# Batch 0's loads ahead of the weights in a one-core linear attention and gated FFN kernel on Trainium2

## The chip, the cores and the metric

The kernel runs on one core of a Trainium2 chip. The metric is the device time of one execution in microseconds (us). Lower is better. Engines: PE is the matmul engine (PEld its weight loads), DVE the vector engine, ACT the scalar engine, POOL GpSimd, SP SyncE. POOL and SP also issue the DMAs here, each through a queue of its own.

## What is computed

```python
def phi(x): return np.where(x > 0, x, np.exp(x) - 1.0) + 1.0
# q, k, v: 8 batches, 8 heads, 576 rows, 64 columns, f32
q_p, k_p = phi(q), phi(k)
kv  = einsum('bhsd,bhse->bhde', k_p, v);  z = sum(k_p, axis=2)
x   = einsum('bhsd,bhde->bhse', q_p, kv) / (einsum('bhsd,bhd->bhs', q_p, z) + 1e-6)
# x is rearranged to 4608 tokens x 512
out = ((x @ w1) * (x @ w2)) @ w3 @ w_out        # w1, w2: 512x1024, w3: 1024x1024, w_out: 1024x512
```

Since nothing nonlinear stands between w3 and w_out, the kernel multiplies them once (the "fold", wf = w3 @ w_out, 1024 x 512) and then computes out = ((x @ w1) * (x @ w2)) @ wf.

## The kernel before

Each of the 576 rows of a batch is either one of 512 "main" rows (four to a partition) or one of 64 remainder rows; the remainder rows of two batches share 128 partitions. There are eight chunks of 512 tokens, one per batch, and a ninth chunk that gathers all remainder rows.

The order of the work is written out by hand: the string ORDER (L451 to L521) lists steps, and a loop at the end of the kernel calls them one after the other. Every engine takes its own instructions in that order and waits only for data and for buffers. A second string, GATES (L523), adds a wait of a load for the landing of another. The steps, with their arguments in the order of the string:

- Loads: ld:n,b,h0,nh,queue loads nh heads of q, k or v of batch b (L117); lr loads the remainder rows of one batch, lp those of two (L124, L132); l3:i loads tile i of w3 (128 rows, L155), lo two of the eight row blocks of w_out (L148), lw:n,x,w a range of columns of w1 or w2 (L141). Weight loads are issued on POOL and turn f32 into bf16 on the way. q, k, v arrive in a pool of five 1 MB buffers, which the two halves of w3 use too. A POOL load waits for the landing of the one eight before it.
- phi: x is the exponential (ACT, L164), t is max(x, 0) + 1 (DVE, L170), m takes the minimum of both (DVE, L177). xr, tr, mr do the same for the remainder.
- Attention of a batch: v and vr copy v to bf16; kv multiplies k and v for a pair of heads (PE, L230); kc and kh copy the result out; qt transposes q on PE and qc copies it out (later batches: qd, a DMA transpose); na multiplies q with kv (PE, L288); nd divides (three DVE instructions, L304); xp and xc transpose the result for the gates (later batches: xd).
- Fold: w3t transposes a tile of w3 on PE (L351), w3c copies it out; wa:c0,n multiplies one block c of all of the first four tiles with w_out (L368), so that four results grow side by side in two attention buffers of PSUM (pool at_ps, two buffers); wf:i does a later tile at once in a buffer of mm_ps (four buffers, L377); wc copies the result to SBUF.
- Gates and output: f:c,f multiplies chunk c with 128 columns of w1 and of w2 (eight matmuls, L397); ac copies the first product out (L405), ab multiplies it with the second (L410); fk does a part of f for the first gate of chunk 0. o:c,m gives 128 rows of the output (eight matmuls, L415), oc copies them out (L422), st stores them (L434); ol is the last output tile, done in two halves (L439). For chunk 8 one st is two stores.
- warm:n runs n matmuls on zeros.

In before the loads of the start stand in this order on POOL: tiles 0 to 3 of w3, w_out, tiles 4 and 5 of w3, then k, q and v of batch 0, tiles 6 and 7 of w3, the first, second and remaining columns of w1 and w2, then batch 1. All of the fold but tiles 6 and 7 is done on PE ahead of batch 0's attention, those two in the middle of it, and the gates of chunk 0 follow.

Of the kernel before, what the change touches and what calls it, by code (L numbers as in the profile page):

```python
# [8 lines left out]
F32 = mybir.dt.float32  # L9
# [4 lines left out]
P = 128  # L14
# [4 lines left out]
def kernel(  # L19
# [11 lines left out]
    nc = tc.nc  # L31
# [4 lines left out]
    FC = DFF // P  # L36
# [10 lines left out]
    ld = ctx.enter_context(tc.tile_pool(name="ld", bufs=5))  # L47
# [327 lines left out]
                ps["wf", i] = o[:, i % 2, :]  # L375

    @step  # L377
    def wf(i):
        o = got(ps, ("wf", i), mm_ps, [P, DM], F32, "mm", "wf_ps")
        for c in range(FC):  # L380
            nc.tensor.matmul(o, sb["w3t", i][:, c, :], sb["wo"][:, c, :],  # L381
                             start=(c == 0), stop=(c == FC - 1))
# [66 lines left out]
                queue.dma_start(out=dst[:, cols], in_=d[r, cols])  # L449

    ORDER = """  # L451
    const:0 const:2 lr:k,0,s const:9 l3:0 lr:v,0,s const:11 l3:1 warm:26,0 const:3 l3:2 l3:3 lo:0,2
    xr:k,0,0 const:6 lo:2,2 const:8 const:7 lo:4,2 zr:0,1 tr:k,0,0 lo:6,2 mr:k,0,0 const:10 l3:4 const:4
    const:1 l3:5 zr:0,0 const:5 w3t:0 ld:k,0,0,4,g warm:8,1 w3c:0,a w3t:1 warm:8,2 w3c:1,v vr:0,a
    ld:k,0,4,4,g w3t:2 warm:8,3 w3c:2,a w3t:3 ld:q,0,0,4,g warm:8,4 w3c:3,a ld:q,0,4,4,g wa:0,1 wa:1,1
    ld:v,0,0,4,g wa:2,1 wa:3,1 ld:v,0,4,2,g wa:4,1 wa:5,1 ld:v,0,6,2,g wa:6,1 l3:6 w3t:5 w3t:4 w3c:5,a
    wa:7,1 l3:7 t:k,0,0,4 w3c:4,a wf:5 wc:2,v wc:3,a wc:1,v lw:0,0,256 wc:0,a t:k,0,4,4 x:k,0,0,4 wf:4
    lw:1,0,256 wc:5,a m:k,0,0,0 m:k,0,0,1 x:q,0,0,4 warm:10,10 t:q,0,0,4 wc:4,a warm:10,11 lw:0,1,256
    m:q,0,0,1 x:q,0,4,4 m:q,0,0,0 warm:10,12 warm:10,13 x:k,0,4,4 lw:1,1,256 v:0,0,4,v qt:0,0,2
    m:k,0,4,3 lw:0,1,512 kv:0,1 qc:0,0,2,a m:k,0,4,2 kv:0,0 v:0,4,2,v lw:1,1,512 kc:0,0,1,0,v v:0,6,2,a  # L460
    kv:0,2 t:q,0,4,4 kc:0,0,1,1,a kh:0,2,1,a kv:0,3 kh:0,2,0,v ld:k,1,0,8,g m:q,0,4,2 na:0,0 kh:0,3,0,a
    w3t:6 kh:0,3,1,v m:q,0,4,3 na:0,1 nd:0,0 qt:0,2,2 ld:q,1,0,8,g w3t:7 w3c:6,v qc:0,2,2,a xp:0,0
    w3c:7,v wf:6 ld:v,1,0,4,g lr:k,1,s xc:0,0,a nd:0,1 lr:v,1,s ld:v,1,4,4,g na:0,3 xp:0,1 wc:6,v na:0,2
    wf:7 nd:0,3 xc:0,1,v nd:0,2 xp:0,3 fk:0,0,0,2 wc:7,v xc:0,3,a xp:0,2 xc:0,2,v fk:0,0,2,1 fk:0,0,3,1
    ac:0,0,a f:0,1 ab:0,0 xr:k,0,1 ac:0,1,a tr:k,0,1 mr:k,0,1 f:0,2 ab:0,1 ac:0,2,a f:0,5 ab:0,2 vr:1,v
    ac:0,5,a f:0,4 ab:0,5 ac:0,4,a t:k,1,0,4 x:k,1,4,4 f:0,6 t:k,1,4,4 x:k,1,0,4 ab:0,4 m:k,1,4,2
    ac:0,6,a f:0,7 m:k,1,0,0 m:k,1,0,1 ab:0,6 x:q,1,0,4 lp:k,1,s t:q,1,0,4 f:0,3 ac:0,7,a m:q,1,0,0
    ld:k,2,0,8,s m:q,1,0,1 v:1,0,4,a m:k,1,4,3 ab:0,7 ac:0,3,a kv:1,1 t:q,1,4,4 qt:1,0,2 x:q,1,4,4
    ab:0,3 kv:1,0 o:0,2 v:1,6,2,a kc:1,0,1,1,v lp:v,1,s m:q,1,4,3 qc:1,0,2,a m:q,1,4,2 kc:1,0,1,0,a
    v:1,4,2,a qt:1,2,2 oc:0,2,v na:1,1 ld:q,2,0,8,s kv:1,2 qc:1,2,2,a st:0,2,g nd:1,1 kv:1,3 o:0,3  # L470
    kh:1,2,1,a kh:1,3,0,a kh:1,3,1,v kh:1,2,0,v ld:v,2,0,8,s xp:1,1 x:k,2,0,4 t:k,2,4,4 na:1,2 na:1,0
    oc:0,3,v o:0,1 xr:k,1,2 nd:1,2 st:0,3,g x:k,2,4,4 ld:k,3,0,8,s nd:1,0 xc:1,1,a na:1,3 xp:1,2
    oc:0,1,a m:k,2,4,3 o:0,0 nd:1,3 xc:1,2,a st:0,1,g tr:k,1,2 vr:3,a t:k,2,0,4 xp:1,3 vr:2,a xp:1,0
# [12 lines left out]
    ac:2,7,a f:2,3 ab:2,7 ld:k,5,0,8,s xr:q,0,2 tr:q,0,2 ac:2,3,a mr:q,0,2 f:2,4 ab:2,3 ac:2,4,a
    lp:k,3,s m:q,4,0,1 na:3,1 m:q,4,4,3 na:3,0 m:q,4,0,0 f:2,6 nd:3,1 ac:2,6,a m:q,4,4,2 ab:2,4
    v:4,4,4,a qd:4 na:3,2 f:2,2 ab:2,6 v:4,0,4,a nd:3,2 ac:2,2,a nd:3,0 f:2,1 ab:2,2 x:k,5,0,4 t:k,5,0,4
    ac:2,1,a kv:4,1 t:k,5,4,4 kv:4,2 lp:v,3,s x:k,5,4,4 kv:4,0 ab:2,1 na:3,3 kv:4,3 nd:3,3 o:2,1
    kc:4,0,2,1,a kc:4,0,2,0,a qdr:0 m:k,5,0,1 m:k,5,4,2 m:k,5,0,0 o:2,2 m:k,5,4,3 xr:k,3,2 xd:3 oc:2,1,v  # L490
    tr:k,3,2 st:2,1,g mr:k,3,2 na:4,2 oc:2,2,v o:2,0 nd:4,2 st:2,2,g na:4,0 oc:2,0,v o:2,3 nd:4,0
    st:2,0,g vr:6,a ld:q,5,0,8,s na:4,1 oc:2,3,v na:4,3 nd:4,3 st:2,3,g f:3,7 nd:4,1 ac:3,7,a xd:4 f:3,3
    ab:3,7 ac:3,3,a f:3,0 ab:3,3 ac:3,0,a nar:1 f:3,4 ab:3,0 ndr:1 x:q,5,0,4 ld:v,5,0,8,s t:q,5,4,4
    f:3,5 ac:3,4,a t:q,5,0,4 x:q,5,4,4 ld:k,6,0,8,s ab:3,4 ac:3,5,a m:q,5,0,0 f:3,2 m:q,5,4,2 ab:3,5
    ac:3,2,a m:q,5,0,1 m:q,5,4,3 f:4,5 qd:5 ab:3,2 ac:4,5,a f:4,0 ab:4,5 v:5,4,4,a v:5,0,4,v ac:4,0,a
    kv:5,0 ab:4,0 kv:5,2 f:4,3 ac:4,3,a t:k,6,4,4 x:k,6,0,4 f:4,6 t:k,6,0,4 ab:4,3 x:k,6,4,4 ac:4,6,a
    kv:5,3 nar:0 kv:5,1 ab:4,6 f:3,6 kc:5,0,2,0,a m:k,6,4,3 vr:7,a kc:5,0,2,1,v m:k,6,4,2 ac:3,6,a
    m:k,6,0,0 m:k,6,0,1 na:5,2 ld:v,6,0,8,s f:3,1 ndr:0 nd:5,2 xdr:0 ac:3,1,a ab:3,6 na:5,0 na:5,1 f:4,7
    nd:5,0 nd:5,1 ac:4,7,a na:5,3 ab:3,1 ld:q,6,0,8,s f:4,4 nd:5,3 ld:k,7,0,8,s v:6,0,4,a ab:4,7 xd:5
    o:3,1 ac:4,4,a v:6,4,4,a ab:4,4 kv:6,1 oc:3,1,a o:3,0 st:3,1,g x:q,6,4,4 t:q,6,0,4 o:3,2 t:q,6,4,4  # L500
    oc:3,0,a m:q,6,4,3 x:q,6,0,4 m:q,6,4,2 st:3,0,g kv:6,0 oc:3,2,v kv:6,3 kv:6,2 x:k,7,0,4 ld:q,7,0,8,s
    m:q,6,0,0 o:3,3 st:3,2,g m:q,6,0,1 t:k,7,0,4 qd:6 kc:6,0,2,0,a kc:6,0,2,1,a x:k,7,4,4 m:k,7,0,1
    m:k,7,0,0 f:4,1 oc:3,3,v t:k,7,4,4 st:3,3,g ac:4,1,a m:k,7,4,2 f:4,2 m:k,7,4,3 ab:4,1 ac:4,2,a
    ab:4,2 f:5,5 ac:5,5,a o:4,0 ab:5,5 f:5,2 oc:4,0,v x:q,7,4,4 lp:q,1,s t:q,7,4,4 st:4,0,g ac:5,2,a
    t:q,7,0,4 x:q,7,0,4 f:5,3 ab:5,2 ac:5,3,a f:5,4 ab:5,3 ac:5,4,a m:q,7,0,1 lp:q,2,s m:q,7,4,3 na:6,3
    m:q,7,0,0 na:6,1 ab:5,4 o:4,1 lp:q,3,s nd:6,1 m:q,7,4,2 ld:v,7,0,8,s nd:6,3 f:5,0 qd:7 oc:4,1,v
    ac:5,0,a st:4,1,g na:6,0 o:4,2 ab:5,0 nd:6,0 o:4,3 oc:4,2,a st:4,2,g na:6,2 v:7,0,4,a f:5,7 tr:q,1,2
    nd:6,2 oc:4,3,a v:7,4,4,a xd:6 st:4,3,g kv:7,1 kv:7,0 ac:5,7,a f:5,1 xr:q,1,2 ab:5,7 ac:5,1,a
    mr:q,1,2 xr:q,2,2 tr:q,2,2 kv:7,3 ab:5,1 kv:7,2 f:5,6 kc:7,0,2,1,a kc:7,0,2,0,v qdr:1 mr:q,2,2
    ac:5,6,a tr:q,3,2 xr:q,3,2 na:7,3 qdr:2 na:7,0 ab:5,6 o:5,0 nd:7,0 nd:7,3 o:5,1 oc:5,0,a st:5,0,g  # L510
    f:6,1 oc:5,1,a st:5,1,g ac:6,1,a f:6,0 ab:6,1 ac:6,0,a na:7,1 f:6,3 ab:6,0 nd:7,1 ac:6,3,a o:5,3
    mr:q,3,2 ab:6,3 nar:5 oc:5,3,a nar:4 f:6,6 ndr:5 st:5,3,g ndr:4 ac:6,6,a nar:2 xdr:2 na:7,2 ab:6,6
    f:6,7 nd:7,2 ac:6,7,a ndr:2 xd:7 f:6,4 ab:6,7 ac:6,4,a o:5,2 ab:6,4 nar:3 oc:5,2,a f:6,5 qdr:3 ndr:3
    st:5,2,g ac:6,5,a xdr:1 f:6,2 ab:6,5 ac:6,2,a f:7,4 ab:6,2 ac:7,4,a f:7,0 ab:7,4 ac:7,0,a o:6,0
    ab:7,0 nar:7 oc:6,0,v nar:6 o:6,3 ndr:7 st:6,0,g ndr:6 f:7,7 oc:6,3,a xdr:3 st:6,3,g ac:7,7,a o:6,2
    ab:7,7 f:7,3 oc:6,2,v st:6,2,g ac:7,3,a f:7,6 ab:7,3 ac:7,6,a f:7,5 ab:7,6 ac:7,5,a f:7,2 ab:7,5
    ac:7,2,a f:8,5 ab:7,2 ac:8,5,a f:8,6 ab:8,5 ac:8,6,a f:8,3 ab:8,6 ac:8,3,a f:8,2 ab:8,3 ac:8,2,a
    f:8,1 ab:8,2 ac:8,1,a f:8,0 ab:8,1 ac:8,0,a f:8,4 ab:8,0 ac:8,4,a f:8,7 ab:8,4 ac:8,7,a o:6,1 ab:8,7
    o:8,2 oc:6,1,a st:6,1,g o:8,3 oc:8,2,a st:8,2,s o:8,0 oc:8,3,v st:8,3,s f:7,1 oc:8,0,a st:8,0,s
    ac:7,1,a o:8,1 ab:7,1 o:7,1 oc:8,1,v st:8,1,s o:7,2 oc:7,1,v st:7,1,s o:7,0 oc:7,2,a st:7,2,s ol:7,3  # L520
    oc:7,0,v st:7,0,s  # L521
# [41 lines left out]
```

## Time and profile before

| | |
|---|---|
| Median of 4 runs | 255.34 us (254.66 to 255.47) |
| The profiled execution | 254.66 us, its span 252.9 us |
| PE busy | 237.4 us, 94% of the span |
| DVE, ACT, POOL busy | 164.5, 125.4, 37.4 us |
| DMA | 50.06 MB, mean 198 GB/s |
| Mean granted PE clock | 0.997 |

The profile is of one execution; its times are counted from the start of the span. What it gives as the time of a group is the sum over its instructions. A row of the timeline has the start, the duration, the engine, the line of the source, the operation, output and inputs, and in brackets the idle time ahead of it and what ended it. The time from issue to landing of a DMA includes its time in the queue. [...]

### The profile page before, as it was taken

The numbers are of one execution on the slowest core, as the hardware profiler recorded it, in microseconds if no ns is written. First come the engines' busy times: TensorE is split into PE (matmuls) and PEld (weight loads), VectorE is DVE, ScalarE is ACT, GpSimd is POOL, SyncE is SP. The second block draws the span as 40 slices with busy tenths as digits, with TensorE's granted clock in tenths as the row PEclk, the third lists the DMA queues.
The fourth block names the chain that finished last, engine by engine and source line by source line (L and its number), as shares of the span: only waits on it lengthen the run. The fifth ranks groups of instructions, "written<-read, shape, count | busy, mean of one in ns | idle before, by whom it ended". The sixth has DMA issues, their size and how long they took to land.

```text
span 252.9 us, 4031 instructions
## 1 busy us (share of the span) xinstructions
PE 237.4 (94%) x1482; PEld 126.8 (50%) x1498; DVE 164.5 (65%) x364; ACT 125.4 (50%) x190; POOL 37.4 (15%) x63
## 2 busy tenths in 40 slices
PE   4899789999899999999999999999999999999993
PEld 4855654456355554544455454445454444444442
DVE  7405787799975997997868875866567454343131
ACT  3327724698966976832665674437332322333200
POOL 8644720002100200011000020110100011000000
PEclk9999999999999999999999999999999999999998
DMA  6999999999999999999995999999307513000543
GB/s 121 206 277 346 203 200 313 280 233 343 318 240 266 293 239 334 203 177 297 239 276 165 270 286 263 191 295 167 109 16 106 125 42 104 3 0 0 128 121 124
DMA packets 69363, 50.06 MB, mean 198 GB/s; under 512 B 41312, under 2 KB 64096, under 8 KB 69344
## 3 DMA queue, kind: packets, MB, share of 16 engines
q1 hardware_dynamic: 59840, 30.81, 54.9%
q0 software_dynamic: 9360, 18.88, 28.4%
q8 instruction: 11, 0.18, 0.3%
q10 hardware_dynamic: 144, 0.13, 0.2%
q14 instruction: 8, 0.07, 0.1%
HBM read 38.80 MB, written 9.44 MB: 191 GB/s over the span
## 4 chain that ended last, share of the span: by engine, by line
PE 73%; DVE 14%; ACT 5%; issue 4%; POOL 2%; DVEq 0%; ACTq 0%; POOLq 0%
PE a_ps L393 21%; PE b_ps L393 20%; PE o_ps L418 19%; PE wa L373 3%; DVE xn L299 3%; ACT e L166 2%; PE kvp L238 2%; DVE t L172 2%; DVE ab L412 2%; PE w3p L356 2%; PE nd L291 2%; DVE k L180 2%; DVE q L180 1%; PE wf_ps L381 1%; DVE r L298 1%
## 5 line engine op out<-in xcount | busy, mean ns | idle before, releaser
L393 PEld LDWEIGHTS <-w_sb 128*128 128x128 bf16 x576 | 55.5, 98 | 64.8 <-DVE xt L338 1.4
L412 DVE TENSOR_TENSOR ab<-a_sb,b_ps 128x512 bf16<-128x512 f32 x72 | 49.1, 684 | 41.3 <-PE b_ps L393 36.4
L407 ACT COPY a_sb<-a_ps 128x512 f32<-128x512 f32 x72 | 42.1, 585 | 63.8 <-PE a_ps L393 62.1
L393 PE MATMUL a_ps<-xt,w_sb 128*128 128x512 bf16 x256 | 66.0, 379 | 1.8 <-DVE xt L338 1.8
L393 PE MATMUL b_ps<-xt,w_sb 128*128 128x512 bf16 x256 | 66.0, 379 | 0.0
L418 PE MATMUL o_ps<-wf_sb,ab 128*128 128x512 bf16 x267 | 63.7, 379 | 0.9 <-DVE r L297 0.3
L436 POOL DMA_DIRECT2D out_dram<-o_sb x28 | 15.7, 561 | 185.3 <-ACT o_sb L424 105.1
L418 PEld LDWEIGHTS <-ab 128*128 128x128 bf16 x280 | 26.6, 98 | 29.5 <-DVE ab L412 0.9
L424 ACT COPY o_sb<-o_ps 128x512 f32<-128x512 f32 x18 | 10.5, 585 | 27.6 <-PE o_ps L418 27.5
L299 DVE TENSOR_TENSOR xn<-nd,r 128x512 bf16<-128x512 f32 x32 | 22.1, 691 | 1.1
L424 DVE COPY o_sb<-o_ps 128x512 f32<-128x512 f32 x17 | 11.7, 688 | 11.2 <-PE o_ps L418 11.2
L166 ACT ACTIVATE e<-q 128x1024 bf16<-128x1024 f32 x16 | 16.9, 1060 | 2.0 <-DVE k L180 1.2
L172 DVE TENSOR_SCALAR t<-k 128x1024 bf16<-128x1024 f32 x16 | 10.7, 688 | 10.0 <-DMA k<-in_k_dram 10.0
L166 ACT ACTIVATE e<-k 128x1024 bf16<-128x1024 f32 x16 | 16.6, 1055 | 0.9 <-DMA k<-in_k_dram 0.9
L217 ACT CAST vt<-v 128x1024 bf16<-128x1024 f32 (+1 forms) x15 | 14.3, 970 | 0.7 <-DMA v<-in_v_dram 0.7
L180 DVE TENSOR_TENSOR k<-t,e 128x512 bf16<-128x512 bf16 x32 | 12.1, 419 | 2.7 <-ACT e L166 2.3
L238 PE MATMUL kvp<-vt,k 128*128 128x130 bf16 x128 | 11.1, 220 | 1.8 <-DVE kvb L248 1.3
L180 DVE TENSOR_TENSOR q<-t,e 128x512 bf16<-128x512 bf16 x32 | 12.2, 419 | 0.7 <-ACT e L166 0.2
L291 PE MATMUL nd<-kvb,qt 128*128 128x130 bf16 x128 | 11.4, 220 | 1.0 <-DVE xn L299 0.6
L291 PEld LDWEIGHTS <-qt 128*128 128x128 bf16 x128 | 8.9, 98 | 5.5 <-DVE xn L299 0.7
L238 PEld LDWEIGHTS <-k 128*128 128x128 bf16 x128 | 9.1, 98 | 4.6 <-issue 1.0
L172 DVE TENSOR_SCALAR t<-q 128x1024 bf16<-128x1024 f32 x16 | 10.7, 690 | 0.5 <-DMA q<-in_q_dram 0.5
(69 smaller groups left out, 195.5 us busy)
## 6 DMA issues: line engine op xcount, KB each, us to landing
out_dram<-o_sb POOLq DMA_DIRECT2D x28, 256.0 KB, 5.4
k<-in_k_dram SPq DMA_DIRECT2D x6, 1024.0 KB, 9.0
q<-in_q_dram SPq DMA_DIRECT2D x6, 1024.0 KB, 8.7
v<-in_v_dram SPq DMA_DIRECT2D x6, 1024.0 KB, 7.4
w3b<-in_moe_w_dram POOLq DMA_DIRECT2D x8, 256.0 KB, 8.2
v<-in_v_dram POOLq DMA_DIRECT2D x3, 512.0 KB, 18.5
out_dram<-o_sb SPq DMA_DIRECT2D x9, 128.0 KB, 2.3
k32r<-in_k_dram SPq DMA_DIRECT2D x8, 128.0 KB, 9.4
```

The source lines that it names most:

```text
L166: return nc.scalar.activation(out=e[:, 0:nh * W], in_=raw[n, b][:, h0 * W:(h0 + nh) * W], func=AF.Exp)
L172: nc.vector.tensor_scalar(out=d[:, 0:nh * W], in0=raw[n, b][:, h0 * W:(h0 + nh) * W], scalar1=0.0, scalar2=1.0, op0=ALU.max, op1=ALU.add)
L180: nc.vector.tensor_tensor(out=d[:, hp].rearrange("p j u d -> p u j d"), in0=ts[n, b, h0][:, s].rearrange("p (u j d) -> p u j d", u=2, j=NJ ...
L238: nc.tensor.matmul(dst, kj[:, hp, j].rearrange("p u d -> p (u d)"), vt[:, j, 2 * hp:2 * hp + 2, :].rearrange("p h e -> p (h e)"), start=(j ...
L291: nc.tensor.matmul(o[:, j // 2, (j % 2) * 256:(j % 2) * 256 + PW], sb["qt", b][:, hp, j * P:(j + 1) * P], kvb[b][:, hp].rearrange("p u e - ...
L299: nc.vector.tensor_tensor(out=dst, in0=o[:, :, :, 0:D], in1=r.unsqueeze(3).to_broadcast(list(r.shape) + [D]), op=ALU.mult)
L393: nc.tensor.matmul(o, w[:, kc, f * P:(f + 1) * P], xt_of(c)[:, :, kc, :], start=(kc == 0), stop=(kc == KC - 1))
L407: return copy_of[eng](out=d, in_=ps["a", c, f])
L412: nc.vector.tensor_mul(out=d[:, f, :], in0=sb["a", c, f], in1=ps["b", c, f])
L418: nc.tensor.matmul(d, sb["ab", c][:, f, m * P:(m + 1) * P], wf_sb[:, f, :], start=(f == 0), stop=(f == FC - 1))
L424: return copy_of[eng](out=d, in_=ps["o", c, m])
L436: queue_of[queue].dma_start(out=dst, in_=sb["o", c, m][r])
```

## The change

The order of the string ORDER is replaced as a whole, and a step wb is added.

1. k, q and v of batch 0 are issued first on POOL, ahead of all weights. The weights follow: tiles 0 to 3 of w3, w_out, tiles 4 and 5, the first columns of w1 and w2, tile 6, the second columns, tile 7, the remaining columns.
2. Batch 0's attention stands ahead of the fold on PE.
3. The fold of the first four tiles is no longer done with wa but with single matmuls wb:i,c (tile i, block c) in an order of their own: first blocks 0 and 1 of several tiles, then the later blocks.
4. Tiles 6 and 7 are transposed between gate steps of chunk 0, and wf:7, wf:5 and wf:6 stand behind four gate steps of it.
5. Warm matmuls: 76 instead of 98. On DVE six memsets of kv buffers now stand ahead of that of zero.
6. Everything behind it is put in a new order too: batch 2 is loaded v, q, k instead of k, q, v; some copies change between ACT and DVE; the last full output tile is o:8,0 (copied by ACT, behind the halves of ol) instead of o:7,0 (copied by DVE).

```diff
+    @step
+    def wb(i, c):
+        o = got(ps, ("wa", i // 2), at_ps, [P, 2, 512], F32, "at", "wa")
+        nc.tensor.matmul(o[:, i % 2, :], sb["w3t", i][:, c, :], sb["wo"][:, c, :],
+                         start=(c == 0), stop=(c == FC - 1))
+        ps["wf", i] = o[:, i % 2, :]
     ORDER = """
-    const:0 const:2 lr:k,0,s const:9 l3:0 lr:v,0,s const:11 l3:1 warm:26,0 const:3 l3:2 l3:3 lo:0,2
-    xr:k,0,0 const:6 lo:2,2 const:8 const:7 lo:4,2 zr:0,1 tr:k,0,0 lo:6,2 mr:k,0,0 const:10 l3:4 const:4
-    const:1 l3:5 zr:0,0 const:5 w3t:0 ld:k,0,0,4,g warm:8,1 w3c:0,a w3t:1 warm:8,2 w3c:1,v vr:0,a
...
-    ab:7,0 nar:7 oc:6,0,v nar:6 o:6,3 ndr:7 st:6,0,g ndr:6 f:7,7 oc:6,3,a xdr:3 st:6,3,g ac:7,7,a o:6,2
...
-    ac:7,1,a o:8,1 ab:7,1 o:7,1 oc:8,1,v st:8,1,s o:7,2 oc:7,1,v st:7,1,s o:7,0 oc:7,2,a st:7,2,s ol:7,3
-    oc:7,0,v st:7,0,s
+    const:11 lr:k,0,s ld:k,0,0,4,g const:9 lr:v,0,s const:4 ld:k,0,4,4,g const:7 ld:q,0,0,4,g const:10
+    ld:q,0,4,4,g const:6 xr:k,0,0 const:1 ld:v,0,0,4,g tr:k,0,0 mr:k,0,0 ld:v,0,4,2,g const:8
+    ld:v,0,6,2,g zr:0,1 const:0 l3:0 const:3 warm:26,0 x:k,0,0,4 l3:1 t:k,0,0,4 l3:2 x:k,0,4,4 m:k,0,0,1
...
+    lw:0,0,256 w3t:2 nd:0,1 na:0,0 xp:0,3 w3c:2,a lw:1,0,256 xc:0,3,v w3t:3 nd:0,0 l3:6 wb:2,0 w3c:3,v
+    wb:1,0 wb:0,0 wb:2,1 xc:0,2,v wb:3,0 wb:1,1 lw:0,1,256 xp:0,0 wb:2,2 wb:2,3 xc:0,0,v wb:3,1 wb:3,2
+    wb:1,2 lw:1,1,256 wb:1,3 wb:1,4 wb:1,5 wb:2,4 wb:2,5 xp:0,1 wb:0,1 wb:0,2 xc:0,1,v wb:3,3 wb:3,4
+    l3:7 wb:3,5 wb:3,6 wb:1,6 wb:1,7 wb:3,7 wb:2,6 wc:1,v lw:0,1,512 wb:2,7 wc:3,a w3t:4 wc:2,v wb:0,3
+    wb:0,4 w3c:4,a wb:0,5 lw:1,1,512 w3t:5 wb:0,6 wb:0,7 w3c:5,a wf:4 wc:0,v ld:k,1,0,8,g lr:k,1,s
+    lr:v,1,s ld:q,1,0,8,g f:0,1 wc:4,a ld:v,1,0,4,g ac:0,1,a w3t:6 ab:0,1 fk:0,0,0,2 ld:v,1,4,4,g
+    w3c:6,a fk:0,0,2,1 fk:0,0,3,1 f:0,3 ac:0,0,a ab:0,0 ac:0,3,a w3t:7 ab:0,3 f:0,2 w3c:7,a tr:k,0,1
+    ac:0,2,a xr:k,0,1 wf:7 ab:0,2 mr:k,0,1 wf:5 wc:7,a vr:1,v wf:6 wc:5,a f:0,5 wc:6,a ac:0,5,a
+    x:k,1,4,4 t:k,1,0,4 f:0,4 t:k,1,4,4 x:k,1,0,4 ab:0,5 f:0,6 m:k,1,4,3 ac:0,4,a m:k,1,0,0 m:k,1,4,2
+    ab:0,4 ac:0,6,a ld:v,2,0,8,s x:q,1,4,4 lp:v,1,s m:k,1,0,1 f:0,7 ab:0,6 x:q,1,0,4 t:q,1,4,4 m:q,1,4,3
+    v:1,0,4,a m:q,1,4,2 t:q,1,0,4 qt:1,2,2 v:1,4,2,a m:q,1,0,0 kv:1,1 m:q,1,0,1 kv:1,0 qc:1,2,2,a
+    v:1,6,2,v kv:1,2 qt:1,0,2 kc:1,0,1,1,a lp:k,1,s kh:1,2,1,v kc:1,0,1,0,a kh:1,2,0,v kv:1,3 ac:0,7,a
+    na:1,2 kh:1,3,1,v qc:1,0,2,a ab:0,7 o:0,0 nd:1,2 kh:1,3,0,a ld:q,2,0,8,s v:2,0,4,v na:1,0 oc:0,0,a
...
+    st:7,2,s o:8,2 oc:8,3,v st:8,3,s o:8,0 oc:8,2,v st:8,2,s ol:7,3 oc:8,0,a st:8,0,s
```

In GATES the same loads are gated as before, in another order: the remainder loads and batch 2's loads on SP wait for q of batch 1, lr:k,1 for the first columns of w1.

## The prediction

> **What bounds the kernel.** I read the page's slices first: DMA.
>
> ```profile
> DMA  6999999999999999999995999999307513000543
> GB/s 121 206 277 346 203 200 313 280 233 343 318 240 266 293 239 334 203 177 297 239 276 165 270 286 263 191 295 167 109 16 106 125 42 104 3 0 0 128 121 124
> ```
>
> One slice is 6.3 us. The DMA engines are taken from the first slice to the 28th, about 180 us; the written rate is near 200 GB/s where the weights are cast on the way (slices 2, 5, 6) and near 345 where f32 comes in as it is (slice 4). So the start is a race for transfers. Next, busy time by stage:
>
> ```profile
> 20.70:41.30 20.60, 17.37 (x170) 11.38 (x169) 15.23 (x37) 11.79 (x19) 8.76 (x11) 1.00 1.21 250
> 41.30:53.40 12.10, 12.10 (x58) 5.50 (x57) 9.36 (x19) 8.79 (x14) 0.00 (x0) 1.00 0.89 263
> 53.40:65.74 12.34, 10.98 (x99) 6.76 (x99) 11.55 (x30) 11.20 (x19) 1.65 (x3) 1.00 1.12 326
> ```
>
> Columns: stretch, its length, busy us of PE, PEld, DVE, ACT, POOL, clock, DMA share, GB/s. From 41.3 PE is full; 53.4 to 65.7 lacks 1.4 us; from 65.74 to 240 the same view gives 1.3 us idle in all. So PE bounds everything behind 41 us, and only three places can pay: the start, the passage through batch 1 (53 to 66), and the end. The timeline of PE names what stands there:
>
> ```profile
> 8.36 1.06 PE L113 MATMUL warm<-zero 128*128 128x128 bf16 x8
> ...
> 13.09 0.61 PE L113 MATMUL warm<-zero 128*128 128x128 bf16 x8
> 13.53 6.39 PE L373 MATMUL wa<-wo,w3A 128*128 128x512 bf16 x27
> ...
> 53.38 0.39 PE L238 MATMUL kvp<-vt,k 128*128 128x130 bf16 x4
> ...
> 65.74 1.04 PE L393 MATMUL a_ps<-xt,w_sb 128*128 128x512 bf16 x4 [1.26 <-DVE xt L338]
> ```
>
> Start to start, a 512-column matmul takes 0.216 us (four in 0.86), so a gate step f or an output step o is 8 x 0.216 = 1.73; eight 128-column ones take 0.85 at 8.4 us and 0.44 at 13.1; a kv step 0.28, an na or xp step 0.22, a qt step 0.45. Last, DMA rows, each from a window that holds one issue (size, then us from issue to landing):
>
> ```profile
> wo<-in_moe_w_out_dram POOLq DMA_DIRECT2D x1, 256.0 KB, 7.6
> w_sb<-in_moe_w_dram POOLq DMA_DIRECT2D x1, 512.0 KB, 14.0
> k<-in_k_dram POOLq DMA_DIRECT2D x1, 1024.0 KB, 16.1
> q<-in_q_dram POOLq DMA_DIRECT2D x1, 1024.0 KB, 17.9
> v<-in_v_dram POOLq DMA_DIRECT2D x1, 512.0 KB, 18.5
> ```
>
> With their issues (3.5, 28.0, 29.2, 30.8, 31.8): first piece of w_out 11.1, last columns of w1/w2 42.0, batch 1's k 45.3, q 48.7, v 50.3; v's second half (32.9 + 19.5) 52.4.
>
> **The change, part by part.**
>
> *Transfers.* k, q, v of batch 0 are 3 MB. In before, successive 512 KB pieces land at 20.1 and 21.6, so 1.5 us each, 9.0 us in all; a 256 KB weight piece takes 1.35 (landings 31.2, 32.6). Put ahead, they delay w_out's first piece from 11.1 to 20.1 (I take 20.5). Behind it, the first gate columns have all but the last two w3 pieces ahead, so they land 2 x 1.35 earlier: 28.5 and 29.9; the second columns 32.6 and 33.9; the last w3 piece 35.2. The bytes up to the last columns are the same: 42.0. Batch 1's loads stay behind them: 45.3, 48.7, 50.3, 52.4.
>
> *Batch 0's attention* moves under the weights. From k's landing (about 5.3, as the first piece in before, 1.3 + 3.9) to v's (about 13) and on through exp 1.06, max 0.69, four m steps, qt, qc 1.0, kv, na and 1.1 us each for four nd steps it is done by about 22; its xt is first read by f:0,1 near 30. Cost nothing, cover 8 us. The six 0.52 us memsets now ahead of zero delay the warm-up by 5 us, but it waits for nothing and holds up only qt, inside the same cover. 22 warm matmuls fewer: 1.2 to 2.4 us of PE time that was idle anyway.
>
> *The fold and the first gates on PE.* From 20.5: 32 wb + 32 wf + four gate pairs' 32 matmuls = 96 x 0.216 = 20.7; w3t 4 to 7, 4 x 0.45 = 1.8; two xp 0.4. Sum 22.9, so f:0,5 starts at 43.4. wb comes in the order in which w_out's pieces land (1.35 apart for 8 matmuls of 1.73), so after the first one PE is the later; f:0,1 falls at 30 (columns 29.9), f:0,3 at 34 (33.9), f:0,5 at 43.4 (42.0): no wait. Before has the same work done (fold, four pairs) at 41.30 + 3 x 1.73 = 46.5. **Gain 3.1 us.** The time comes out of the waits and warm matmuls between 25 and 41.
>
> *What is late next: batch 1.* PE ends f:0,7 at 50.4, three us earlier than before (53.38), but batch 1's q and v come no earlier. On DVE from k's landing: two t 1.3, three m 1.2, ab:0,5 0.6, ab:0,4 0.6, m 0.4, ab:0,6 0.6, t and two m twice 2.8, v 0.4, three kh 0.5, ab:0,7 0.6 = 9.0, so ab:0,7 ends at 54.3 or 55 (ACT has ac:0,7 behind two v copies, qc and two kc). PE has 2.2 us of qt, kv and na to put there and starts o:0,0 at 54.2, of which only the last matmul needs ab:0,7. Before had this PE work (without o:0,2, which it slips in between) done at 57.57 - 1.73 = 55.8. Left: 1.6 us. The four o steps, three na and four xp then take 8.4, and with two waits for nd of 0.3 and 0.6 the gates of chunk 1 start at about 63.5 against 65.74: **2.2 us** ahead, since before idles 1.4 us there.
>
> Bounds for this wait: without the remainder load that before issues at 32.6 among the weights (128 KB), v may land 1 us earlier; with ld:v,2 issued on SP as soon as q lands (48.7), in before only at 49.5, v's last half may be 1 us later. I take neither.
>
> *The middle, replanned throughout.* Same instructions, other order. ACT now has x:k,2, x:k,3 and x:q,3 directly ahead of ac steps, and batch 2 is loaded v, q, k instead of k, q, v. In before k of batch 3 landed at 56.1 + 14.3 = 70.4 and q at 63.0 + 12.7 = 75.7; in after I get ACT to them at 71 and 74.5. So a stall between 0 and the whole lead of 2.2; below nothing too, since 1.3 us of idle could vanish. I take 0.5 loss, from the 0.9 to 1.2 us by which q is late.
>
> *The end.*
>
> ```profile
> 248.26 0.68 DVE L424 COPY o_sb<-o_ps 128x512 f32<-128x512 f32 x1
> 248.37 0.33 SPq L449 DMA_DIRECT2D out_dram<-o_sb  x1
> 248.79 0.37 ACT L447 COPY o_sb<-o_ps 128x256 f32<-128x256 f32 x1 [2.84 <-PE o_ps L445]
> 248.97 0.33 SPq L436 DMA_DIRECT2D out_dram<-o_sb  x1
> ```
>
> In before the last full copy (oc:7,0) is on DVE and overlaps PE's last half; ACT's half copy ends at 249.16 and its store is issued at 249.19, landing 2.4 later. In after oc:8,0 is on ACT, behind that half copy and its 0.37 us store issue: 249.56 + 0.59 = 250.15, then two SP issues of 0.33 (chunk 8's rows go in two stores), landing 2.3 after the second: 252.8 against 251.6. **Loss 1.1** (0.9 to 1.3).
>
> Sum: -3.1 + 1.5 - 0.6 + 0.5 + 1.1 = **-0.6 us**. On the profiled execution (254.66, span 252.9) 254.1; that execution was the lowest of four, so on the median of 255.34 I forecast **254.7**.
>
> [...] PE idles or trickles from about 13 to 20.5. In before, the trickle from 27.99 to 34.31 (55 matmuls, busy share 0.59) left the matmuls at 34.3 at full pace, while behind the idle 4.1 to 7.5 they took 0.107 us for 128 columns until 12.6, with the clock column at 1.00 throughout. After's trickle has some 92 matmuls in 7.5 us, so I take full pace.
> [...]
>
> **Rivals.** (1) The lead is kept: loads of batches 2 and 3 arrive in time and the middle's idle shrinks by half a us: -2.2 - 0.5 + 1.1 = -1.6, 253.7 (253.0 to 254.4). For it: DMA is no fuller than before. Chance 0.28. (2) PE is at half pace when wb starts: at most 5 us of it (7.55 to 12.6 in before), +2.5 at f:0,5, of which the 1.5 of waiting for batch 1 is absorbed: +1.0, 255.7. Chance 0.10. (3) Slower: loads decide the middle. ACT stands at x:k,2, x:k,3 or x:q,3 until they land, the ac steps behind it keep the four mm_ps buffers, and PE stops about one gate step (1.73) later. It decides once a load lands over 1.7 us after ACT gets there. If the stream is no faster than in before, the whole lead of 2.2 goes: +1.1; with batch 2's k third instead of first (4 us per MB) up to 1.5 more: +2.6. Middle 257.1. For it: DMA at 1.12 from 53 to 120, and DVE and ACT over 90% busy in the passage. Against: PE's chunk 1 gates leave 14 us before batch 2 is needed. Chance 0.27.
>
> **Numbers.** Forecast case 0.35 (254.0 to 255.5). 0.3% of 255.34 is 0.77 us, about what a measurement can tell: faster is below 254.57. Faster: rival 1 and 0.4 of the forecast case, 0.42; same: the rest of it and half of (2), 0.26; slower: (3) and the other half, 0.32. Range 253.0 (rival 1's end) to 257.2.
>
> **To look for.** Right if f:0,5 (first gate with columns over 512) starts near 43.4, PE idles 1 to 2 us between 50 and 54, the gates of chunk 1 start near 63.5, and ACT ends with a 512-column copy after its last store issue. Wrong if w_out's first piece lands after 22, if wb matmuls come 0.43 apart, or if PE idles over 2.5 us from 64 to 130.

## The result and the profile after

| | before | after |
|---|---|---|
| median | 255.37 us (72 runs, 254.21 to 257.35) | 257.07 us (46 runs, 255.11 to 261.9) |
| ratio of after to before | | 1.0051 [1.0038, 1.0065] |
| profiled execution, its span | 254.66, 252.9 us | 257.99, 256.2 us |
| last matmul ends | 248.75 | 250.5 |
| gates of chunk 1 start | 65.74 | 65.16 |
| PE's time lost from 70 us on | 2.76 | 4.90 |

After is slower by 0.5%, where 254.7 was forecast. All ratios here come from undisturbed runs, those within 1.5% of the fastest of their kernel. "PE's time lost" is the sum of what the distances from one matmul's start to the next exceed those of back-to-back matmuls (0.216 us for 512 columns); gaps of exactly one matmul, where a record is missing, are left out. The profiled execution of after lies 0.9 us above its median, that of before 0.7 below its own: of the 3.3 us between them, 1.6 are such scatter.

The chain that ended last, from the page of after. In before no DMA had a share of it that counts; here it has 16%.

```profile
PE 69%; DMA 16%; DVE 7%; ACT 3%; issue 2%; POOL 0%; ACTq 0%; DVEq 0%; POOLq 0%
PE a_ps L400 22%; PE b_ps L400 21%; PE o_ps L425 15%; DMA xt<-xn 8%; DMA qt<-q 6%; DMA k<-in_k_dram 3%; PE wf_ps L388 3%; PE wa L380 3%; PE nd L291 2%; DVE xn L299 2%; PE kvp L238 2%; ACT e L166 1%; DVE r L298 1%; PE w3p L356 1%; PE o_ps L452 1%
```

Busy time by stage in after (columns as in the prediction; the DMA share is that of 16 engines, and one queue alone can be above 1 by it, 1.44 in before from 31.1 to 31.5): fold and first gates, batch 1, the way to chunk 1's gates, and the stretch to 120.

```profile
21.70:45.54 23.84, 22.97 (x134) 11.58 (x138) 8.75 (x17) 9.17 (x13) 7.35 (x10) 1.00 1.22 232
45.54:56.57 11.03, 9.50 (x74) 5.33 (x73) 8.32 (x19) 9.84 (x15) 0.00 (x0) 1.00 1.11 287
56.57:65.16 8.59, 8.49 (x61) 4.71 (x61) 8.03 (x21) 6.00 (x11) 1.87 (x3) 1.00 1.11 304
65.16:120.00 54.84, 52.77 (x325) 27.11 (x327) 46.41 (x107) 32.72 (x50) 4.94 (x9) 1.00 1.13 261
```

Besides 0.9 us in the fold, PE lacks work mainly in two places: 1.5 us around batch 1 and 2.1 us between 65 and 120, where before lacked 1.0 of 54.26. The timeline of PE in after shows the first one, and what held the fold:

```profile
21.70 0.38 PE L380 MATMUL wa<-wo,w3A 128*128 128x512 bf16 x1 [0.24 <-DMA wo<-in_moe_w_out_dram]
22.79 1.25 PE L380 MATMUL wa<-wo,w3A 128*128 128x512 bf16 x4 [0.71 <-DVE xn L299]
...
53.20 0.62 PE L267 MATMUL qtp<-ident,q 128*128 128x128 bf16 x8 [0.59 <-DVE q L180]
...
56.06 0.39 PE L238 MATMUL kvp<-vt,k 128*128 128x130 bf16 x4 [0.94 <-DVE kvb L259]
```

The second place, by the view of PE's waits from the gates of chunk 1 to 170 us. After (columns: who waits for what, total, times, longest):

```profile
PE a_ps L400 <- DMA xt<-xn: 1.4, 2, 0.8
PE kvp L238 <- ACT vt L217: 0.4, 1, 0.4
PE nd L291 <- DMA qt<-q: 0.4, 1, 0.4
PE o_ps L425 <- DVE ab L419: 0.3, 1, 0.3
PE nd L291 <- DVE xnr L299: 0.3, 1, 0.3
```

Before, same view:

```profile
PE a_ps L393 <- DVE xt L338: 1.3, 1, 1.3
PE xtp L333 <- DVE xn L299: 0.6, 1, 0.6
PE nd L291 <- DVE xn L299: 0.6, 1, 0.6
PE o_ps L418 <- DVE r L297: 0.3, 1, 0.3
```

Before waits for DVE, after mostly for DMA transposes and a load (vt is late because v landed only at 104.7). Before's 1.3 us for xt stand directly ahead of its first gate at 65.74, so its middle holds the other three rows alone. The view counts from the modelled end of a matmul and so shows less than the start-to-start sum. The end of after:

```profile
249.67 0.42 DVE L454 COPY o_sb<-o_ps 128x256 f32<-128x256 f32 x1 [1.85 <-PE o_ps L452]
250.12 0.34 SPq L456 DMA_DIRECT2D out_dram<-o_sb  x1
250.54 0.37 ACT L454 COPY o_sb<-o_ps 128x256 f32<-128x256 f32 x1 [11.52 <-PE o_ps L452]
250.94 0.37 ACTq L456 DMA_DIRECT2D out_dram<-o_sb  x1
251.43 0.59 ACT L431 COPY o_sb<-o_ps 128x512 f32<-128x512 f32 x1 [0.52 <-ACT o_sb L454]
252.04 1.11 SPq L443 DMA_DIRECT2D out_dram<-o_sb  x2
```

ACT copies one after the other, and SP then needs 1.11 us for the two stores. From the last matmul to the end of the span: 5.7 us, against 4.1 in before.

### The profile page after: what moved, and what is told of

Read it like the earlier page. It is cut to its first block, busy times and chain, and to the rows that moved or that the text cites. A ratio compares the mean times of both kernels' runs of the same rounds, so it can differ in the third digit from the quotient of the medians.

```text
span 256.2 us, 4002 instructions
## 1 busy us (share of the span) xinstructions
PE 235.8 (92%) x1460; PEld 124.5 (49%) x1476; DVE 168.3 (66%) x371; ACT 120.0 (47%) x183; POOL 37.5 (15%) x63
## 4 chain that ended last, share of the span: by engine, by line
PE 69%; DMA 16%; DVE 7%; ACT 3%; issue 2%; POOL 0%; ACTq 0%; DVEq 0%; POOLq 0%
PE a_ps L400 22%; PE b_ps L400 21%; PE o_ps L425 15%; DMA xt<-xn 8%; DMA qt<-q 6%; DMA k<-in_k_dram 3%; PE wf_ps L388 3%; PE wa L380 3%; PE nd L291 2%; DVE xn L299 2%; PE kvp L238 2%; ACT e L166 1%; DVE r L298 1%; PE w3p L356 1%; PE o_ps L452 1%
## 5 line engine op out<-in xcount | busy, mean ns | idle before, releaser
L431 ACT COPY o_sb<-o_ps 128x512 f32<-128x512 f32 x20 | 11.6, 583 | 24.4 <-PE o_ps L425 23.7
L431 DVE COPY o_sb<-o_ps 128x512 f32<-128x512 f32 x15 | 10.3, 687 | 10.1 <-PE o_ps L425 10.1
L113 PE MATMUL warm<-zero 128*128 128x128 bf16 x76 | 6.8, 279 | 6.4 <-DVE zero L96 6.4
L217 ACT CAST vt<-v 128x1024 bf16<-128x1024 f32 (+1 forms) x10 | 8.9, 921 | 5.6 <-DMA v<-in_v_dram 5.6
```

The source lines that it names most:

```text
L431: return copy_of[eng](out=d, in_=ps["o", c, m])
```

## The experiments

Each run stands beside runs of before on the same chip, and the ratio is to those; 0.001 is 0.26 us.

**The tail.** e1_tail is after with the last full copy ahead of the last tile; e8_before_act_tail gives before the copy of after.

```diff
-    st:8,2,s ol:7,3 oc:8,0,a st:8,0,s          # e1_tail, in after
+    st:8,2,s oc:8,0,a st:8,0,s ol:7,3
-    oc:7,0,v st:7,0,s                          # e8_before_act_tail, in before
+    oc:7,0,a st:7,0,s
```

> The changed kernel with the copy and the store of o:8,0 moved ahead of the step ol, nothing else. By the traces the last store issue falls at 252.04 + 1.11 in the changed kernel, behind ACT's half copy (250.54), its store issue (250.94) and the full copy (251.43). Theory (three separate places, the tail worth 1.6 us): the copy runs under ol's matmuls, the end comes 1.2 to 1.6 us earlier, about 255.6 if the changed kernel is at 257.1. Rival (the tail is only the last of several things that end together, as the store of ol itself lands at 250.9 + 2.4): under 0.5 us gained.

Measured: 255.24, ratio 0.999 [0.9953, 1.0027].

> The kernel before, with its last full copy on ACT instead of DVE, behind ACT's half copy and its store's issue, as in after; the middle and the start are untouched. Theory: the copy starts at about 249.6 and ends at 250.2 instead of 248.9, its store is issued about 1.2 us later and becomes the last to land: 0.9 to 1.2 us slower, 256.1 to 256.4. The rest of the 1.8 that the tail cost in after would then be chunk 8's second store (0.3 to 0.6). Rival, the end is set by the last store to land whichever engine copied: under 0.4 us slower.

Measured: 256.34, 1.0036 [1.0016, 1.0057], 0.9 us, and the end has the form of after's:

```profile
249.35 0.37 ACT L447 COPY o_sb<-o_ps 128x256 f32<-128x256 f32 x1 [2.84 <-PE o_ps L445]
249.75 0.37 ACTq L449 DMA_DIRECT2D out_dram<-o_sb  x1
250.22 0.59 ACT L424 COPY o_sb<-o_ps 128x512 f32<-128x512 f32 x1 [0.49 <-ACT o_sb L447]
250.83 0.33 SPq L436 DMA_DIRECT2D out_dram<-o_sb  x1
```

Both theories held. Four pairs of runs (after and e1, e9 and e11, e15 and e16, e13 and e17) differ in this edit alone: their ratios differ by 0.0061, 0.0046, 0.0054 and 0.0052, on average 1.4 us. 0.9 of it is the copy on ACT. The rest was not tested by itself; by the profiles, in which the stretch behind the last matmul is 4.1 us in before, 5.1 in e8 and 5.7 in after, it is the second store of chunk 8, whose issue row is 0.78 us longer (1.11 against 0.33).

**Halves of the two orders.** Behind the cut the steps not yet done follow in the order of the other kernel.

```diff
# e2_newstart_oldrest: order of after up to f:0,5, then that of before, with its end
# e3_oldstart_newrest: order of before up to f:0,1, then that of after, with its end
```

> The changed kernel's order up to, but not with, f:0,5; from there on the order of before (batch 1's passage, middle and end). Theory: the new start is worth 0.95 us at f:0,5 (45.54 against 46.48), and the loss of 2.1 in the middle and of 1.6 at the end belong to the new order behind it: 0.3 to 1.0 us faster than before, about 254.7. Rival (PE being earlier puts the load stream out of step, whatever the order): PE idles at batch 1 and in the middle as in the changed kernel, 256 to 257.

Measured: 256.88, 1.0042 [1.0013, 1.0071]. The theory fell. The number is the rival's, but PE's waits from 65 to 170 in its profile are mostly for DVE (the longest in total 1.4, 1.3 and 1.1 us), and 0.4 for a DMA transpose.

> The order of before up to, but not with, f:0,1 (old loads, old fold); from there on the order of the changed kernel. Theory: middle and end lose by themselves, 2.1 + 1.6 and the batch 1 passage a little: 258 to 259.5 against 255.4, slower than the changed kernel by the 0.6 to 1 us that its start is worth. Rival (the middle loses only because PE is early against the loads): only the end is lost, about 257.

Measured: 258.47, 1.0077 [1.0042, 1.0112]. The median lies in the theory's range, the 2.0 us by the ratio between it and the rival's 1.6; the tail explains 1.4 of them. Neither half gains by itself. In e2's profile the gates of chunk 1 start at 66.1 (before 65.74): with before's order of batch 1 nothing is left there of the new start's lead.

**The start and the passage through batch 1.** e4_delay adds 18 warm matmuls ahead of f:0,1; e5_wb_order reorders the fold's first steps; e6_fill moves work into batch 1's wait; e7_all is e5, e6 and the tail's edit.

```diff
-    ld:q,1,0,8,g f:0,1                                            # e4_delay
+    ld:q,1,0,8,g warm:18,20 f:0,1
-    wb:2,0 w3c:3,v wb:1,0 wb:0,0 wb:2,1 xc:0,2,v wb:3,0 wb:1,1    # e5_wb_order
+    w3c:3,a wb:2,0 wb:2,1 wb:3,0 xc:0,2,v wb:1,0 wb:0,0 wb:1,1
-    v:1,0,4,a m:q,1,4,2 t:q,1,0,4 qt:1,2,2                        # e6_fill
+    ac:0,7,a v:1,0,4,a m:q,1,4,2 ab:0,7 t:q,1,0,4 o:0,0 qt:1,2,2
```

> The changed kernel with 18 more matmuls on zeros (1.0 us of PE time) ahead of the first gate step. In the changed kernel's trace the exps of batch 1 start directly behind ac:0,5 and ac:0,6 (47.21, 50.54), though k and q landed at 45.5 and 48.5. Theory (the 1.5 us that PE idles at batch 1 come from the order on ACT and DVE, which moves with PE): +0.8 to +1.0 us on the changed kernel. Rival, that of the prediction (the wait is for batch 1's loads, and swallows what PE loses): +0.0 to +0.3, PE idles 0.5 instead of 1.5 us from 52 to 57.

Measured: 260.52, 1.0181 [1.0129, 1.0233]. PE's waits in batch 1 were the same 1.5 us by the view of waits, so not the loads but the order on ACT and DVE sets them. The size was underrated: by the ratios it is 3.3 us on after. The profile is of the fastest of the six runs; it lost 2.49 us at 114 on a transposed x, where after lost 0.96. Where the rest of the 3.3 us goes stays open.

> The kernel after, with the first six single steps of the fold in another order (blocks 0 and 1 of tile 2 and block 0 of tile 3 first, the copy of tile 3 on ACT): in after the second of them waited 0.7 us for the attention buffer that batch 0's division still held. Theory, the lead of the start is lost to batch 1's order: f:0,5 about 0.7 us earlier (44.8), but batch 1's wait longer by as much and the gates of chunk 1 again near 65.2, time 256.8 to 257.4. Rival, the start's wait is what costs: the gates of chunk 1 near 64.5 and 256.2 to 256.6.

Measured: 257.93, 1.0107 [1.007, 1.0144], above both. In its profile the fold began late, at 23.0, and not early: PE ran at half pace. Its PE alone, in stretches of 3.41 us (busy us and count, clock, DMA share, GB/s):

```profile
12.62:16.04 3.42, 1.62 (x22) 0.98 1.08 258
16.04:19.45 3.41, 2.86 (x29) 0.52 1.13 208
19.45:22.86 3.41, 2.99 (x47) 1.00 1.24 204
```

> The kernel after, with the last gate pair's copy and product of chunk 0 and the output step o:0,0 ahead of batch 1's v copies and q transpose, so that PE has 1.7 us of work where it waits 1.5 us for batch 1. Theory, the wait comes from the order on ACT and DVE: the waits between 52 and 57 us fall from 1.5 to under 0.6 us, the gates of chunk 1 start near 64.3 instead of 65.16, and the time falls by 0.5 to 0.9 if the middle keeps it (256.2 to 256.6), by nothing if the middle takes it back. Rival, the loads of batch 1 set it: the wait moves behind o:0,0 and the gates stay near 65.2, 257.1.

Measured: 258.04, 1.0107 [1.0062, 1.0153], above both; the waits for batch 1 did not fall (1.7 us by the view from 50 to 66, 1.5 in after). The profile is a lucky accident: two half-pace stretches (16.3 and 60.7) put the gates of chunk 1 at 68.65, 3.5 us after those of after, and yet the last matmul ends at 250.6, within 0.1 us of after's. From 70 on PE lost only 1.26 us. Between these two profiles a lead of 3.5 us is worth nothing in after's middle.

```profile
57.28:60.70 3.42, 1.65 (x23) 0.98 1.08 338
60.70:64.11 3.41, 3.41 (x15) 0.52 1.18 292
```

The DMA rows suggest why. SP's rows of the DMA transposes in after:

```profile
67.73 8.28 SPq L279 DMA_TRANSPOSE qt<-q  x1
82.48 8.22 SPq L279 DMA_TRANSPOSE qt<-q  x1
99.59 5.69 SPq L279 DMA_TRANSPOSE qt<-q  x1
105.99 5.60 SPq L343 DMA_TRANSPOSE xt<-xn  x1
```

and in e6_fill:

```profile
71.21 3.56 SPq L279 DMA_TRANSPOSE qt<-q  x1
85.97 4.02 SPq L279 DMA_TRANSPOSE qt<-q  x1
101.36 1.80 SPq L279 DMA_TRANSPOSE qt<-q  x1
107.31 2.79 SPq L343 DMA_TRANSPOSE xt<-xn  x1
```

The second column is how long SP is held. From issue to landing these four took 11.9, 14.9, 7.7, 9.9 us in after and 7.2, 7.5, 4.3, 4.3 in e6: issued later, they landed earlier, the last at 111.6 instead of 115.9. The 1 MB loads just ahead of the three q transposes landed at 76.3, 91.0 and 104.7 in after (DMA rows), and SP came free at 76.0, 90.7 and 105.3; in e6 they landed at 74.6, 88.9 and 101.8, and SP came free at 74.8, 90.0 and 103.2. So these transposes of 512 KB hold SP until about the time at which the load ahead is through. Before's q transposes were held too:

```profile
70.22 5.18 SPq L279 DMA_TRANSPOSE qt<-q  x1
87.85 3.37 SPq L279 DMA_TRANSPOSE qt<-q  x1
101.86 3.97 SPq L279 DMA_TRANSPOSE qt<-q  x1
```

They landed at 77.4, 96.1 and 108.0. After issued them 2.5, 5.4 and 2.3 us earlier and got them at 79.6, 97.3 and 107.3: issued earlier they gain little or nothing, and for the 8.3, 8.2 and 5.7 us of the hold SP issues nothing behind them. Two things limit this. The smaller transposes of the remainder are not held so: the one at 116.4 in after let go of SP at 119.2, though v, issued ahead of it, landed only at 125.2. And a small delay does not bring e6's gain: e11 (below), whose first q transpose was issued at 68.45, 0.7 us behind after's, held its four for 6.4, 7.4, 5.6 and 5.6 us.

> The kernel after with three edits together: the fold's first steps reordered, o:0,0 put into batch 1's wait, and the copy and store of o:8,0 ahead of the last output tile. Theory: the tail gives 1.8 by itself, the start's two edits 0.5 to 1.5, so 253.8 to 254.8, below the kernel before. Rival, the middle takes back what comes early: about 255.2, as with the tail's edit alone.

Measured: 257.19, 1.0069 [1.0039, 1.0099]. Its gates of chunk 1 started at 65.0, and PE lost 5.18 us from 70 on, 2.2 of it by the view of waits on transposed x. The rival's mechanism held, and it took more than the rival said.

**The half-pace stretches.** e9_warm fills the gaps with warm matmuls; e11_tail_warm adds the tail's edit.

```diff
-    qt:0,0,2 ... qt:0,2,2 ... qt:1,2,2 ... na:1,2
+    warm:14,15 qt:0,0,2 ... warm:16,16 qt:0,2,2 ... warm:8,17 qt:1,2,2 ... warm:10,18 na:1,2
```

> The kernel after, with 48 more warm matmuls in PE's gaps: 14 and 16 ahead of batch 0's two q transposes, 8 and 10 ahead of batch 1's first q transpose and first na. In three of the seven profiles so far that have the new start PE ran at half pace for one stretch of 3.4 us from about 16.0 (granted clock 0.50), after a stretch of 3.41 us with 1.62 to 1.84 us of PE work, and the fold began 1.4 us later in them; stretches with 1.93 us or more were followed by full pace. Theory, such half-pace stretches are part of the loss, and chance sets them: no 0.50 in the clock ahead of 65 us, first fold matmul at 21.7 in this profile, the runs less spread (256 to 258), median 256.3 to 256.9. Rival, the DMA stream of the middle sets the end whatever the start does: 257.0 to 257.3, as after.

Measured: 257.92, 1.0095 [1.0063, 1.0127].

> The kernel after with the 48 warm matmuls and with the copy and store of o:8,0 ahead of the last output tile. Theory (half-pace stretches cost): 254.3 to 254.9, runs from 253.7 to 256, where the tail's edit alone gave 255.24 with runs from 254.0 to 260.3. Rival (the stream of the middle): 255.2, the same spread.

Measured: 256.6 (255.01 to 259.88), 1.0049 [1.0018, 1.0081]. The stretches were gone from both profiles, and neither time nor spread got better: runs of e11 with a mean clock of 1.0 took 255.0 to 258.5. The theory fell, though the 48 matmuls are work of their own (e11 is 1.5 us behind e1). After's own runs say the same: the 14 that enter its ratio with a mean clock of 0.998 or more have a median of 256.6, still 1.3 above before. Half pace comes and goes from run to run (the mean clock of after's runs is 0.985 to 0.999), but it is not what makes after slow. It is part of the spread: in e1 the five runs with such a clock took 254.0 to 256.3, the other seven up to 260.3.

**The stream of the middle.** e10_gate holds three transposes until the load ahead of them has landed; e12_tail_warm_gate adds the tail and the warm matmuls. e13_after_half_v and e14_before_half_v load half of v for three batches (the other heads use that half too, so the result is not the full one). e15_pe_transposes does two q transposes on PE; e16_tail_pe_transposes adds the tail's edit.

```diff
-        nc.sync.dma_start(out=d.rearrange(...), ..., transpose=True)         # e10: qd returns it,
+        return nc.sync.dma_start(out=d.rearrange(...), ..., transpose=True)  # and GATES gets
+    qd:2<ld:q,3,0,8,s qd:3<ld:q,4,0,8,s qd:4<ld:v,4,0,8,s
-    ld:v,3,0,8,s ld:v,4,0,8,s ld:v,5,0,8,s                                   # e13, e14
+    ld:v,3,0,4,s ld:v,4,0,4,s ld:v,5,0,4,s
-    qd:2 ... f:1,1 ... qd:3 ... f:2,1                                        # e15
+    qt:2,0,2 qc:2,0,2,a qt:2,2,2 qc:2,2,2,v f:1,1 ... qt:3,0,2 qc:3,0,2,a qt:3,2,2 qc:3,2,2,v f:2,1
```

> The kernel after, with the DMA transposes of q of batches 2, 3 and 4 held on SP until the load issued just ahead of them has landed (q of batch 3, q of batch 4, v of batch 4). In after they were issued into running loads and took 8.3, 8.2 and 5.7 us; in the run whose PE was 3.4 us later they took 3.6, 4.0 and 1.8 us and ended 1.3 us earlier. Theory, transposes that run beside loads make the stream of the middle late: they take 3.5 to 4.5 us each, the waits of PE at 96 to 115 us fall from 2.8 to under 1.5, and the time by 0.5 to 1.3, to 255.8 to 256.6. Rival, the stream is bound by its bytes and the hold only moves the time: waits as before or 0.5 to 1 us more, 257 to 258.

Measured: 266.21, 1.0412 [1.038, 1.0444]. The theory's first half held, its sum did not: the transposes now took 1.8 us of SP and 4.3 us to land, but SP's waits for the loads (first fence) left the 16 engines nearly idle, as the stretch from 74 to 76 shows (second fence: share 0.08).

```profile
SPq L279 <- DMA q<-in_q_dram: 20.5, 2, 10.5
SPq L279 <- DMA v<-in_v_dram: 4.7, 1, 4.7
```

```profile
74.00:76.00 2.00, 2.00 (x11) 0.88 (x9) 1.97 (x4) 2.00 (x4) 0.00 (x0) 1.00 0.08 25
```

Holding SP for these 25 us made the kernel 9.1 us slower than after: nothing in the middle hides a pause of the stream. Part of the 9.1 is a clock of 0.50 behind these waits, in its profile from 88.4 to 95.3 and from 122.6 to 126.0.

> All three edits: the tail, the warm matmuls, the held transposes. If each is worth what its theory says, 253.3 to 254.3, below the kernel before. If the hold only moves the time, 255 or more.

Measured: 263.05, 1.0273 [1.0235, 1.0311], the same lesson.

> The kernel after with only heads 0 to 3 of v loaded for batches 3, 4 and 5 (1.5 MB of 50 less); heads 4 to 7 of these batches use heads 0 to 3 in their place. All instructions stay but the three loads are half as long. Theory, the DMA stream sets the middle: the waits of PE at 105 (v) and 115 (transposed x) go, 2 to 3 us of waits from 96 to 165, and the time falls by 1.5 to 2.5, to 254.6 to 255.6, with less spread. Rival, the order on ACT and DVE sets it: 256.8 to 257.2.

Measured: 254.92 (254.19 to 256.66), 0.9983 [0.9957, 1.0009]. The theory held, in time and spread. PE lost 0.92 us from 70 on instead of 4.90, and this is all that the view of its waits from 65 to 170 has left:

```profile
PE nd L291 <- DVE xnr L299: 0.3, 1, 0.3
```

> The same halves of v left out in the kernel before. Theory: its transposes and loads land with some us in hand there, so little to gain, 0 to 0.5 us: 254.8 to 255.3. Rival, the stream bounds both orders alike: 253.0 to 254.0.

Measured: 254.85, 0.9973 [0.9946, 0.9999], 0.7 us (0.0 to 1.4), a little above the range. Before's PE lost 2.92 us as it had (2.76): its waits are for DVE, and the profile's span stayed at 252.9.

> The kernel after with q of batches 2 and 3 transposed on PE (two qt and two copies each, ahead of f:1,1 and f:2,1) instead of by DMA. PE has 1.8 us more to do; SP has two transposes of 8 us less and the loads behind them start earlier. Theory (stream): the 2.8 us of waits at 96 to 115 go and PE pays 1.8, so 255.8 to 256.8. Rival (order): 258.5 to 259.5, PE's 1.8 on top.

Measured: 258.34, 1.0102 [1.0064, 1.0141]. The theory fell; the value lies just below the rival's. The waits at 96 to 115 did go, but PE paid its 1.8 us and 1.1 more for buffers, and the x of chunk 5 was late instead:

```profile
PE a_ps L400 <- ACT qt L273: 1.1, 1, 1.1
PE a_ps L400 <- DMA xt<-xn: 1.0, 1, 1.0
```

> The same with the copy and store of o:8,0 ahead of the last output tile: 1.5 to 1.8 less than the run without it. Theory: 254.0 to 255.2. Rival: 256.8 to 257.6.

Measured: 256.84, 1.0048 [1.0019, 1.0076], the rival's value.

**Do the terms add up?** e17 is e13 with the tail's edit; e18 the same with before's order up to f:0,1 (the cut of e3).

```diff
# e17_new_start_half_v_tail: v halves of e13 + tail of e1, in after
# e18_old_start_half_v_tail: v halves of e13 + tail of e1, in e3_oldstart_newrest
```

> The kernel after with half of v for batches 3 to 5 left out (as before: heads 4 to 7 use heads 0 to 3) and the copy and store of o:8,0 ahead of the last output tile. If the terms add up: 257.07 less 2.15 (half v) less 1.8 (tail) is 253.1, range 252.8 to 253.6. If the two overlap: 254 or more.

Measured: 253.59 (252.77 to 255.27), 0.9931 [0.9898, 0.9965]: they add up, at the edge of the range.

> The kernel before up to f:0,1, the order of after behind it, with the same halves of v left out and the same tail. Its chunk 1 gates started 0.85 us later than those of after in the profile of the same order without these two edits. If the start's lead at the gates of chunk 1 is what the new start is worth: 0.6 to 0.9 us slower than the run with the new start, 253.7 to 254.2. If the new start is worth the 3.1 us of the forecast's first step: 256.2. If nothing: the same.

Measured: 255.42, 0.9989 [0.9966, 1.0013]. 1.5 us by the ratios, more than the lead; the two intervals leave 0.4 to 2.5 us. Its profile has the gates of chunk 1 at 65.4 (65.0 in e17) and 1.7 us more lost from 70 on, at 160 to 165, on kv copies, a division and a transposed x. Why those are later with the old start stays open.

## Why the prediction was wrong

Forecast: start 2.2 us ahead at the gates of chunk 1, middle 0.5 lost, tail 1.1 lost, sum -0.6. Measured by the ratios: +1.3, of which the tail is 1.4. So start and middle together gave nothing, where 1.7 us were forecast. **The step that failed is "2.2 us ahead" (0.58 in the profiles), and with it the assumption that a lead at chunk 1 is a lead at the end.**

- *Transfers* for the fold and for batch 1 were right within 1.1 us: w_out's first piece at 21.6 (20.5), k, q, v of batch 1 at 45.5, 48.5, 51.5 (45.3, 48.7, 52.4). The first piece took until 7.1, not 5.3, and what follows it up to the first gate columns is later by 0.7 to 2.0.
- *Batch 0's attention, "Cost nothing, cover 8 us"*, failed. The fold's second result shares the two attention buffers with batch 0's division and waited 0.71 us for it; the first matmul waited for w_out, 1.2 us later than forecast. (The warm-up began at 6.35 instead of 1.19, behind seven memsets, not six; nothing waited for it.) f:0,5 started at 45.54, a **gain of 0.95 instead of 3.1**. PE's 22.9 us of work from there on was right (22.97 busy). Over the profiles with this start, f:0,5 lies between 45.1 and 47.3, and the step of equal work between 45.8 and 47.0 with the old one, so 0.95 is uncertain by about as much.
- *"I take full pace"* held for wb. But in three of the twelve profiles with the unchanged start (e1, e5, e6), PE fell to half pace at 16.0 to 16.3 for 3.4 us, and the fold began 1.3 to 1.6 us late. The clock was at 0.50 from 16.3 to 19.7 in e1 and from 16.2 to 19.6 in e6. Cut into stretches of 3.41 us, the profiles show up to 1.84 us of PE work, 54%, ahead of half pace, and no stretch at full pace with 1.93 us (e4, 13.76 to 17.18) or more was followed by it. There is no sharp limit between: e7 stayed at full pace behind 1.82 us (114.75 to 118.16), e6 did not behind 1.84 (12.91 to 16.33). Rival (2) came near to this case, but PE was at full pace again when wb started (in e5 the clock was back at 1.00 from 19.4 on, and the fold began at 23.0); after's median doesn't hang on it.
- *Batch 1*: the wait was predicted, its cause half. "q and v come no earlier" is true, but PE waited 1.5 us for copies and products that stand in line on ACT and DVE (e4: unchanged by a delay of 1 us). Of 0.95 us, 0.58 reached chunk 1: before's 1.4 us of idling there did go, as forecast.
- *The middle, "I take 0.5 loss"*, is by the ratios about right as a number (start 0.58 ahead, nothing left at the end), by luck: in the profiled execution it was 2.3. The 1.3 us of idle that the prediction read in before from 65.74 to 240 are 2.1 in that view (0.96, 0.77 and 0.33). The mechanism was near to rival (3)'s, loads decide, but not at its place: not at the exps of k and q of batches 2 and 3 on ACT, but at DMA transposes of q and x, and at v. (ACT stood 12.0 us for v, q and k from 66 to 170, 2.4 in before, but at later loads, and PE waited only 0.4 for it.) That rival's 257.1 is the measured time by luck too, since its terms were others. Half of three v loads left out brings 1.7 us in after and 0.7 in before; the intervals barely part the two. With the stream relieved and the tail mended, after is 1.1 us (0 to 2.2) ahead of before so relieved (0.9931 against 0.9973): a good part of the 1.7 us forecast for start and middle may be there, and the stream takes it. Whether the bytes or the hold on SP's queue cost it is not shown: e10 and e15, which were to take the hold away, both made the kernel slower.
- *The tail*: mechanism and rows as predicted, the size 1.4 instead of 1.1. The mis-sized term is "two SP issues of 0.33": they took 1.11 us.
- *The argument against rival (3)*, "PE's chunk 1 gates leave 14 us before batch 2 is needed", looked at the loads only. The DMA share of 1.12 from 53 to 120, cited for it, was the row to price, together with SP's rows in before, where the transposes were held for 3.4 to 5.2 us already.

No version that computes everything beat before: after with the tail mended is level with it (0.999).

## What to carry to other kernels

The DMA stream left little slack here (share 1.13 from 65 to 120 in after), and the 0.58 us won ahead of it were lost at its next consumers: before pricing a lead, look for the transfers that land latest before their use, and take their slack as the bound. A DMA transpose of 512 KB issued into running loads held its whole queue (SP for 8.28 us in after, until 76.0, where the load ahead landed at 76.3); and neither half of the new order gained with the other half of the old one. Compare the end of a kernel instruction by instruction: the only certain loss here stood in its last six rows.

## What the runs showed of the hardware

- A DMA transpose of 512 KB held SP's queue for 1.8 us and landed after 4.3 when the load ahead had landed (e10), and took up to 8.3 and 14.9 us behind running loads (after), while nothing else was issued on SP. From issue to landing, 4.3 us for 512 KB are 122 GB/s; a 1 MB load (k at 105.33 in after) took 6.4 us, 164 GB/s. Beside loads the q transposes at 67.7, 82.5 and 99.6 in after took 11.9, 14.9 and 7.7 us.
- PE's clock went to half for 3.4 us after stretches of 3.41 us with 1.57 (e1, 163.08 to 166.49) to 1.84 us of work (e6, 12.91 to 16.33), and with 0.75 in e12 (115.70 to 119.11), not after every such stretch (e7: 1.82), also in the middle (e6 at 60.7) and in before's start (e14 at 30.9). An estimate from these numbers: waits of 1.6 us in all within one stretch can cost up to 1.7 us more.
